# Releasing the first loads of w1 and of batch 1's q by k's features, casting the end of batch 0's v on two engines, and moving batch 7's q transposes, in an attention-and-mixer kernel on one core

## The chip, the core and the metric

The kernel runs on one core of a Trainium2 chip. The core has a matrix engine (TensorE, PE in the profile, with weight loads as PEld), three elementwise engines (VectorE, DVE; ScalarE, ACT; GpSimd, POOL) and an engine that only issues transfers and waits (SyncE, SP). Sixteen DMA engines move data for all of them. The metric is device time in microseconds (us), the median of several runs of the whole kernel.

## What is computed

The reference is a cosine-reweighted linear attention, whose output goes through a low-rank token mixer and a two-layer channel network. Eight batches, eight heads, 576 positions, head width 64, model width 512.

```
r      = relu(x);  phi(x) = [r * cos_w, r * sin_w]       # for q and k, cos_w/sin_w by position
kv     = sum over s of phi(k)[s, f] * v[s, d]            # per batch and head, 128 x 64
z      = sum over s of phi(k)[s, f]
x      = (phi(q) @ kv) / (phi(q) @ z + 1e-6)             # 576 x 512 per batch, heads side by side
u      = x + (x^T @ U @ V)^T                             # rank 32 over the positions
out    = u + relu(u @ w1) @ w2                           # w1 512 x 2048, w2 2048 x 512
```

Inputs and output are float32; the kernel multiplies in bfloat16.

## The kernel before, in words

**Tiles.** A batch's 576 positions are laid out nine to a pair of partitions, so that four chunks of 128 rows and one tail of 64 rows (chunk 4) come from two loads: the odd partitions' rows (`load_odd`, L80 in the profile) and the even partitions' rows with the tail (`load_even`, L74). q, k and v of a batch have one float32 staging tile each (`qst`, `kst`, `vst`), which the next batch's load overwrites. A `*_prep` turns a staged chunk into the two halves of its features (`scaled_relu`, L305 on ScalarE and L307 on VectorE).

**Order.** The order of the instructions on each engine is that of the program text; waits come from the data. Batch 0 is written out by hand. It runs q's features and their transposes on TensorE, k's features with the sums `z` (L1215), and then `first_chain` (L1269): casts of v to bfloat16, `kv` by pairs of heads (`kv0_mm`, L353, heads 0 to 3; `kv_unit`, L341, heads 4 to 7), the denominators (`den_mm`, L1223), the normalised x, the low-rank update and the transposed u. Multiplications with zeros fill TensorE's idle time at the start (`keep_warm`, L202). After that come numbered slots, each holding a unit of TensorE's work of the channel network; the attention work of the following batches is hung beside the slots (`beside`, `attention_plan`). `starts[b]` is the first slot of batch b.

**Loads around the change.** SyncE first issues batch 0's q, k and v, v in two halves of four heads. GpSimd issues the weights: w1 in four quarters of 512 columns (`w1_load`, L102; quarter n serves the hidden blocks 4n to 4n + 3), w2 likewise (`w2_load`, L108), each cast to bfloat16 on the way. A transfer is held back by a mark: a tiny copy that reads a tile, placed ahead of the transfer on the same engine, so that the engine waits until that tile is written.

- L1352, on GpSimd: reads q's tail features (`q_tl`); behind it w1's first quarter.
- L1354, on SyncE: a two-byte transfer that reads chunk 0 of k's cosine features; behind it batch 1's q.
- L1358, on GpSimd: reads the transposed tail of q; behind it w1's other quarters.
- L1361, on SyncE: reads `z_sb`; behind it batch 1's k and v.
- L1380, on GpSimd, slot 6: reads batch 1's transposed q; behind it w2.

After `first_chain` the channel network begins with six multiplications with w1's first quarter (`g1_open`, L727), then `g1_main` (L710). Between them batch 1's q is featured (`q_prep(1, ...)`) and transposed on TensorE (`qtr_unit`, L382).

**Later batches.** From batch 2 on q and u are transposed by the DMA engines, issued from SyncE: `qtr_dma` (L413 for the tail, L408 for two chunks at a time) and `utr_dma` (L535 for two quarters of u at a time, L541 for the tails). In `attention_plan(b)` F is the slot at which the features of batch b begin, G is `starts[b - 1]`, `at_q` gives the slots of the three transposes of q (tail, chunks 0 and 1, chunks 2 and 3), and `u_at + 2` and `u_at + 4` those of u. For batch 7, F is the first slot of batch 5's product with w2; batch 6's u is formed and its transposes are issued beside the same product. `uT_form` (L608) is VectorE's first use of a transposed u, `x_unit` (L439) TensorE's use of a transposed q.

Of the kernel before, what the change touches and what calls it, by code (L numbers as in the profile page):

```python
# [17 lines left out]
def kernel(  # L18
# [11 lines left out]
    nc = tc.nc  # L30

    B = 8
    H = 8
# [15 lines left out]
    def tail(b):  # L49
# [16 lines left out]
    qst, kst, vst = (  # L66
        pool.tile([P, H, 5, D], FP32, tag=n, bufs=1, name=n) for n in ("qst", "kst", "vst")
    )
# [43 lines left out]
    def cast(eng, o, i):  # L112
        if eng is nc.scalar:
            nc.scalar.activation(out=o, in_=i, func=AF.Copy, bias=0.0, scale=1.0)  # L114
        else:
            eng.tensor_copy(out=o, in_=i)  # L116


    V_, A_, G_ = nc.vector, nc.scalar, nc.gpsimd
# [15 lines left out]
    v0 = pool.tile([P, H, 5, D], BF16, tag="hid", bufs=1, name="v0")  # L135

    def load_uv():
# [16 lines left out]
        out=iota[:, 0:4], pattern=[[2, 4]], base=0, channel_multiplier=9,  # L154
        allow_small_or_imprecise_dtypes=True,
    )
    for lo in (0, TS):
        nc.gpsimd.iota(
            out=iota[lo : lo + TS, 4:5], pattern=[[1, 1]], base=8, channel_multiplier=18,
# [3 lines left out]
        out=iota[:, 5:6], pattern=[[1, 1]], base=8, channel_multiplier=9,  # L163
# [6 lines left out]
        out=par, in_=ident[:, 1:P:2], op=ALU.add, axis=mybir.AxisListType.X  # L170
# [14 lines left out]
    q_tl = const.tile([P, H, 2 * D], BF16)  # L185
# [943 lines left out]
    def attention_plan(b):  # L1129
        plan = []  # L1130
        odd = b % 2 == 1

        def put(at, f, *a):
            plan.append((at, lambda: f(b, *a)))

        ops = [(f, c, i) for f in (q_prep, k_prep) for c in QORD for i in range(2)]
        if b == 2:
            for n, (f, c, i) in enumerate(ops):
                if n < 8:
                    put((25, 26, 27, 28, 28, 29, 29, 30)[n], feature, f, c, i, A_)  # L1140
                elif n < 10:
                    put(24 + n, feature, f, c, i, V_)
                else:
                    put(
                        (34, 34, 35, 36, 37, 38, 39, 39, 40, 41)[n - 10], feature, f, c, i,
                        A_ if n in (14, 17) else V_,
                    )
            V0 = 33
            at_q, at_load = (32, 34, 36), (37, 42, 43)
            kv_at, x_at, a_at, u_at = 43, (44, 46, 48, 50, 52), 54, 55  # L1150
            a_bank = O1
        else:
            F, G = starts[b - 2] + (20 if odd and b < B - 1 else 16), starts[b - 1]
            late = b in (4, 6)
            both = (0, 1, 2, 8) if late else (0, 1, 2, 10, 11, 12) if b > 3 else (1, 2, 10, 11, 12)
            for s_ in range(G - F + 2 * late):
                for eng in (A_, V_)[: 1 + (s_ in both)]:
                    if ops:
                        put(F + s_, feature, *ops.pop(0), eng)
            V0 = starts[b - 2] + 9 if b > 3 else F + 1  # L1160
            at_q, at_load = (F + 7, F + 8, F + 8) if late else (F + 5, F + 7, F + 7), (F + 8, F + (16 if late else 14), V0 + (8 if late else 5))
            if b == 6:
                at_q, at_load = (F + 7, F + 12, F + 12), (F + 12, F + 16, V0 + 8)
            if b == 3:
                at_q = (F + 6, F + 7, F + 8)
                at_load = (F + 11, F + 14, F + 14)
            X0 = G - 2 if odd else G
            x_at = [
                X0 + i for i in ((2, 4, 6, 9, 11) if b == 3 else (2, 4, 6, 8, 10) if odd else (3, 5, 7, 9, 11))
            ]  # L1170
            kv_at = X0
            if late:
                kv_at, x_at = G + 3, [G + i for i in (5, 8, 13, 16, 18)]
            elif b - 1 in FULL:
                kv_at, x_at = G + 1, [G + i for i in ODDX]
            elif b - 1 in MIXED:
                kv_at, x_at = G + 1, [G + i for i in X5]
            a_at = x_at[4] + (3 if b in (4, 6) else 2)
            u_at = a_at + 1
            a_bank = T1 if b == 3 else OB  # L1180
        for n, c in enumerate(QORD):
            put(V0 + n, v_prep, 0, H, (c,), (G_,))
        for at_, (c0, c1) in zip(at_q, ((4, 5), (0, 2), (2, 4))):
            put(at_, qtr_dma, c0, c1)
        put(kv_at, kv_pair, *X1)
        for n, c in enumerate(ORD):
            put(x_at[n], x_unit, c, *((O1, X1)[n % 2] if b < 4 else X1))
        put(a_at, A_unit, *a_bank, A_)
        put(u_at, u_va, (0, *X1), (2, *O1) if b < 4 else (2, OA, OB))
        d0 = 2 if odd and b - 1 in FULL else 0  # L1190
        put(u_at, u_add, d0)
        put(u_at + 2, u_add, 2 - d0)
        put(u_at + 2, utr_dma, d0, d0 + 2)
        put(u_at + 4, utr_dma, 2 - d0, 4 - d0)
        if odd:
            late_t = 3 if b == 5 and b - 1 in FULL else 0 if b - 1 in FULL else 1 if b - 1 in MIXED else 0
            put(*((u_at + 1, u_tail, *T1) if b < 4 else (u_at + 3 + d0 + late_t, u_tail, *X1S)))
            put(u_at + 4 + d0 + late_t, utr_dma, 4, 5)
        if b < B - 1:
            for at_, t in zip(at_load, loads(b + 1)):  # L1200
                plan.append((at_, t))
        return plan
# [17 lines left out]
    def den_mm(b, d, cs):  # L1220
        for c in cs:
            for h in range(H):
                nc.tensor.matmul(  # L1223
                    out=d[:, c, h, :], lhsT=qT_of(b, c, h),
                    rhs=z_sb[:, h : h + 1].to_broadcast([P, 12]), start=True, stop=True,
                )
# [42 lines left out]
    def first_chain(b, xz, z, v_ps):  # L1269
        def fill(n):  # L1270
            for _ in range(n):
                nc.tensor.matmul(
                    out=xz[:, 1, P:512], lhsT=zero[:, 0:P], rhs=zero[:, 0:384],
                    start=True, stop=True,
                )

        d = xz[:, 1, 0:480].rearrange("p (c h n) -> p c h n", h=H, n=12)
        rec = pool.tile([P, 5, H], FP32, tag="rec5", bufs=1, name="rec5")
        cast(V_, v0[:, 0:2], vst[:, 0:2])
        cast(V_, z_sb, z[:, :, 0])  # L1280
        cast(V_, v0[:, 2:4], vst[:, 2:4])
        cast(V_, v0[:, 4:H], vst[:, 4:H])
        qtr_evac(b, 4, A_, t_q[4])
        kv_sb[b] = pool.tile([P, H, E], BF16, tag="kv", bufs=2, name="kv")
        acc = bank([P, 4, D], FP32, *G3, "kv_ps")
        kv0_mm(b, acc, (0, 1))
        den_mm(b, d, (0, 1, 2))
        kv0_mm(b, acc, (2, 3))
        cast(A_, V_bf, v_ps.rearrange("r (c p) -> r c p", c=4))
        cast(A_, kv_sb[b][:, 0:4, 0:D], acc)  # L1290
        den_mm(b, d, (3, 4))
        recip(rec, d[:, :, :, 0])
        x0 = [xh_mm(b, c, 0, *G3) for c in ORD[0:2]]
        kv_unit(b, 1, *T1, A_)
        x0 += [xh_mm(b, c, 0, *t) for c, t in zip(ORD[2:5], (G3, OA, OB))]
        xh_norm_act(b, ORD[4], 0, rec, x0[4])
        for n in range(4):
            xh_norm(b, ORD[n], 0, rec, x0[n])
        x1 = [xh_mm(b, c, 4, *t) for c, t in zip(ORD[0:4], (G3, G3, G3, T1))]
        for n in range(2):  # L1300
            xh_norm(b, ORD[n], 4, rec, x1[n])
        uT_alloc(b)
        a_ps = xz[:, 1, 0:P]
        a_mm(b, a_ps, (0, 1), range(5))
        cast(A_, A_of(b)[0:TS, :], a_ps[0:TS, :])
        for i, (tag, bufs) in enumerate((OA, OB, T1)):
            uT_ps[b, i] = bank([P, 4, P], FP32, tag, bufs, "uT_ps")
        for i in range(2):
            open_mm(b, i, uT_ps[b, i], range(4))
        x1.append(xh_mm(b, ORD[4], 4, *G3))  # L1310
        for n in range(2, 5):
            xh_norm(b, ORD[n], 4, rec, x1[n])
        for i in range(2):
            uTd_mm(b, i)
        for i in range(2):
            uTd_evac(b, i, A_)
        a2 = bank([P, P], FP32, *G3, "a_ps")
        a_mm(b, a2, (2, 3), range(5))
        cast(V_, A_of(b)[TS:P, :], a2[TS:P, :])
        open_mm(b, 2, uT_ps[b, 2], range(4))  # L1320
        u3 = ps.tile([P, 2, 512], FP32, tag="X", bufs=1, name="u3")
        uT_ps[b, 3] = u3[:, 0, :].rearrange("p (c t) -> p c t", c=4)
        open_mm(b, 3, uT_ps[b, 3], range(4))
# [25 lines left out]
        z_mm(0, c, z)  # L1349
    qtr_evac(0, 3, A_, t_q[3])  # L1350

    G_.tensor_copy(out=mark[0:1], in_=q_tl[0:1, 0, 0:1])  # L1352
    w1_load(0)
    nc.sync.dma_start(out=mark2, in_=k_p[0][0:1, 0, 0, 0:1])  # L1354
    load_odd(qst, q, 1)
    load_even(qst, q, 1)
    first_chain(0, xz, z, v_ps)
# [136 lines left out]
```

## Time and profile before

| what | us |
|---|---|
| three runs | 290.35, 290.05, 291.34 |
| median | 290.35 |
| profiled execution | 290.51 |
| its span in the profile | 288.7 |
| busy: TensorE, VectorE, ScalarE, GpSimd | 283.0, 218.9, 175.5, 70.9 |

The profile is of one execution; its span runs from the first to the last instruction that the profile counts, and the execution's own time is 1.8 us longer. Rows of a timeline give the start, the busy time, the engine (SPq is the transfer queue that SyncE feeds), the line, the operation, the tile written and the tile read, the shapes and how many instructions were merged; a bracket gives idle time of the engine before it and what ended it. Rows of a DMA queue give packets, megabytes and the packets' time as a share of sixteen engines over the window. The granted TensorE clock was 0.999 of full speed.

### The profile page before, as it was taken

The page shows a single profiled execution, that of the slowest core. Times are in us where ns is not written, and L with a number is a line of the kernel's source. Part 1 is how long each engine was busy: PE and PEld are TensorE (multiplying, and loading weights), DVE is VectorE, ACT ScalarE, POOL GpSimd, SP SyncE. Part 2 cuts the span into 40 slices and gives each one's busy share as a digit, 9 for nine tenths or more (in the row PEclk, how much of TensorE's full clock was granted, in tenths as well). Part 3 has the DMA queues.
Part 4 walks back from the last instruction along what each step waited for, and adds up shares of the span by engine and source line. Part 5 has one row for each costly group of instructions (what it writes and reads, how often), then busy time and mean ns, then how long its engine had stood idle before and what let it go on. Part 6 is the DMA issues. An engine that isn't in the chain of part 4 may idle for free.

```text
span 288.7 us, 7553 instructions
## 1 busy us (share of the span) xinstructions
PE 283.0 (98%) x3110; PEld 209.6 (73%) x3110; DVE 218.9 (76%) x446; ACT 175.5 (61%) x308; POOL 70.9 (25%) x111
## 2 busy tenths in 40 slices
PE   8999999999999999999999999999999999999995
PEld 6776455545887646886887667876888778899884
DVE  4979738887886677558895388958898689689864
ACT  2955661476687366986587488776795772177110
POOL 8340600040045304441006500351006000400140
PEclk9999999999999999999999999999999999999999
DMA  6999999999959898899829993599978200620023
GB/s 197 339 284 253 287 209 259 276 211 176 299 156 177 226 360 174 212 275 299 218 38 185 298 290 105 61 213 207 260 141 147 93 1 8 150 83 2 0 88 132
DMA packets 85447, 53.32 MB, mean 185 GB/s; under 512 B 53990, under 2 KB 83078, under 8 KB 85414
## 3 DMA queue, kind: packets, MB, share of 16 engines
q1 hardware_dynamic: 78998, 41.62, 60.0%
q0 software_dynamic: 6272, 11.17, 16.2%
q8 instruction: 24, 0.39, 0.6%
q10 hardware_dynamic: 144, 0.07, 0.1%
q14 instruction: 9, 0.07, 0.1%
HBM read 36.86 MB, written 9.44 MB: 160 GB/s over the span
## 4 chain that ended last, share of the span: by engine, by line
PE 92%; DMA 3%; DVE 2%; SPq 1%; issue 0%; DVEq 0%
PE w_ps L892 30%; PE g_ps L710 24%; PE al_ps L653 7%; PE be_ps L653 5%; PE gt_ps L741 5%; PE o_ps L781 5%; DMA vst<-in_v_dram 3%; PE x_ps L439 3%; PE kv_ps L364 3%; PE ot_ps L801 2%; PE ot_ps L994 2%; PE a_ps L465 1%; PE va_ps L495 1%; PE t_ps L382 1%; PE g_ps L727 0%; PE va_ps L518 0%
## 5 line engine op out<-in xcount | busy, mean ns | idle before, releaser
L710 PE MATMUL g_ps<-uT,w_bf 128*128 128x512 bf16 x314 | 77.0, 379 | 0.0
L717 ACT ACTIVATE hid<-g_ps 128x512 bf16<-128x512 f32 x80 | 47.4, 597 | 31.8 <-PE g_ps L710 26.6
L912 POOL TENSOR_TENSOR o_sb<-o_sb,u_bf 128x512 f32<-128x512 f32 x21 | 26.2, 1259 | 111.9 <-DVE o_sb L912 111.9
L710 PEld LDWEIGHTS <-w_bf 128*128 128x128 bf16 x314 | 29.1, 98 | 25.9
L892 PEld LDWEIGHTS <-hid 128*128 128x128 bf16 x448 | 43.1, 98 | 5.6 <-DVE hid L857 0.2
L678 DVE TENSOR_TENSOR hid<-pw,be_ps 128x512 bf16<-128x512 f32 x36 | 24.7, 686 | 17.0 <-PE be_ps L653 10.0
L892 PEld LDWEIGHTS <-S 128*128 128x128 bf16 x336 | 32.2, 98 | 4.5
L114 ACT ACTIVATE pw<-al_ps 128x512 f32<-128x512 f32 x36 | 21.3, 595 | 16.5 <-PE al_ps L653 8.9
L892 PE MATMUL w_ps<-T,hid 128*128 128x256 bf16 x224 | 27.9, 273 | 0.0
L892 PE MATMUL w_ps<-w_bf,hid 128*128 128x256 bf16 x224 | 27.6, 273 | 0.0
L892 PE MATMUL w_ps<-T,S 128*128 128x256 bf16 x224 | 27.1, 273 | 0.0
L114 ACT ACTIVATE o_sb<-w_ps 128x512 f32<-128x512 f32 x21 | 12.5, 597 | 20.5 <-PE w_ps L892 14.1
L912 DVE TENSOR_TENSOR o_sb<-o_sb,w_ps 128x512 f32<-128x512 f32 x21 | 14.3, 683 | 12.0 <-ACT o_sb L114 7.6
L506 DVE TENSOR_TENSOR u_bf<-x_bf,va_ps 128x1024 bf16<-128x1024 bf16 (+1 forms) x20 | 19.5, 998 | 3.4 <-PE va_ps L495 2.7
L653 PEld LDWEIGHTS <-sa 128*128 128x128 bf16 x192 | 17.7, 98 | 4.0 <-issue 0.2
L449 DVE TENSOR_TENSOR x_bf<-x_ps,rec 128x512 bf16<-128x512 f32 x28 | 19.3, 691 | 1.0
L305 ACT ACTIVATE k_p<-kst,sinw 128x512 bf16<-128x512 f32 x26 | 17.8, 713 | 0.1
L653 PEld LDWEIGHTS <-w_bf 128*128 128x128 bf16 x144 | 14.0, 98 | 3.5
L116 POOL CAST v_ext<-vst 128x512 bf16<-128x512 f32 x24 | 14.7, 652 | 7.1 <-issue 3.2
L741 PE MATMUL gt_ps<-uT_tl,w_bf 128*128 128x128 bf16 x256 | 16.4, 219 | 0.0
L781 PE MATMUL o_ps<-w_bf,hid 128*128 128x512 bf16 x64 | 15.6, 379 | 0.0
L741 PEld LDWEIGHTS <-w_bf 128*128 128x128 bf16 x256 | 15.0, 98 | 0.4
(191 smaller groups left out, 499.9 us busy)
## 6 DMA issues: line engine op xcount, KB each, us to landing
qst<-in_q_dram SPq DMA_DIRECT2D x14, 512.0 KB, 6.8
kst<-in_k_dram SPq DMA_DIRECT2D x14, 512.0 KB, 8.6
vst<-in_v_dram SPq DMA_DIRECT2D x12, 512.0 KB, 8.4
out_dram<-o_sb POOLq DMA_DIRECT2D x12, 512.0 KB, 5.4
w_bf<-in_moe_w_ch_dram POOLq DMA_DIRECT2D x8, 512.0 KB, 10.9
out_dram<-o_sb SPq DMA_DIRECT2D x4, 512.0 KB, 3.0
qst<-in_q_dram SPq DMA_DIRECT2D x2, 640.0 KB, 5.9
kst<-in_k_dram SPq DMA_DIRECT2D x2, 640.0 KB, 13.6
```

The source lines that it names most:

```text
L114: nc.scalar.activation(out=o, in_=i, func=AF.Copy, bias=0.0, scale=1.0)
L305: nc.scalar.activation(out=o, in_=i, func=AF.Relu, bias=0.0, scale=w)
L449: nc.vector.tensor_tensor(out=x_of(b, c, rows).rearrange("p (g i d) -> p g i d", g=2, d=D), in0=view[:, :, :, 0:D], in1=rec[rows].unsqueez ...
L506: nc.vector.tensor_tensor(out=u_bf[b][:, d0 : d0 + n], in0=x_bf[b].rearrange("p c (d n) -> p d c n", n=P)[:, d0 : d0 + n], in1=t.rearrange ...
L653: nc.tensor.matmul(out=res[:, k_, :], lhsT=lhs[:, d, k_, :], rhs=rhs[:, d, :], start=(opens and k_ == 0 and d == 0), stop=(k_ == 1 and d = ...
L678: V_.tensor_tensor(out=o, in0=x, in1=res, op=ALU.add)
L710: nc.tensor.matmul(out=g_ps.rearrange("p (c t) -> p c t", c=4), lhsT=w1_bf[:, d, j * P : j * P + P], rhs=uT[b][:, d, :, :], start=(d == 0) ...
L717: nc.scalar.activation(out=hid[b][:, j, :], in_=g_ps, func=AF.Relu, bias=0.0, scale=1.0)
L741: nc.tensor.matmul(out=g_ps[:, jj, :], lhsT=w1_bf[:, d, j * P : j * P + P], rhs=uT_tl[pr][:, d, :], start=(d == 0), stop=(d == 3),)
L781: nc.tensor.matmul(out=o, lhsT=hid[0][:, j, cc * P : cc * P + P], rhs=w2_bf[:, j, :], start=(j == 0), stop=(j == NJ - 1),)
L892: nc.tensor.matmul(out=res[:, g, :], lhsT=lhs[:, k_, g * P : g * P + P], rhs=rhs[:, k_, :], start=(opens and k_ == 0 and g == 0), stop=(k_ ...
L912: eng.tensor_tensor(out=o_, in0=x, in1=y, op=ALU.add)
```

## The change

Four edits:

1. In `first_chain`, VectorE casts heads 4 and 5 of batch 0's v; heads 6 and 7 are cast by ScalarE, after its copy of `kv` for heads 0 to 3 and ahead of its copy for heads 4 to 7.
2. The mark ahead of w1's first quarter reads chunk 0 of k's cosine features instead of q's tail features.
3. The mark ahead of batch 1's q reads chunk 1 of k's cosine features instead of chunk 0.
4. For batch 7 the transposes of q's four chunks are issued at slot F + 11 instead of F + 7; on SyncE they come behind the two transposes of batch 6's u instead of ahead of them. The transpose of q's tail stays at F + 5.

The numbers of instructions on TensorE, VectorE, GpSimd and SyncE stay; ScalarE has one more.

```diff
             at_q, at_load = (F + 7, F + 8, F + 8) if late else (F + 5, F + 7, F + 7), ...
+            if b == 7:
+                at_q = (F + 5, F + 11, F + 11)
             if b == 6:
...
     def first_chain(b, xz, z, v_ps):
...
         cast(V_, v0[:, 2:4], vst[:, 2:4])
-        cast(V_, v0[:, 4:H], vst[:, 4:H])
+        cast(V_, v0[:, 4:6], vst[:, 4:6])
         qtr_evac(b, 4, A_, t_q[4])
...
         cast(A_, kv_sb[b][:, 0:4, 0:D], acc)
+        cast(A_, v0[:, 6:H], vst[:, 6:H])
         den_mm(b, d, (3, 4))
...
-    G_.tensor_copy(out=mark[0:1], in_=q_tl[0:1, 0, 0:1])
+    G_.tensor_copy(out=mark[0:1], in_=k_p[0][0:1, 0, 0, 0:1])
     w1_load(0)
-    nc.sync.dma_start(out=mark2, in_=k_p[0][0:1, 0, 0, 0:1])
+    nc.sync.dma_start(out=mark2, in_=k_p[0][0:1, 1, 0, 0:1])
     load_odd(qst, q, 1)
     load_even(qst, q, 1)
     first_chain(0, xz, z, v_ps)
```

## The prediction

> **What bounds the kernel now.** I read the page first, then who waited on TensorE, the chain that ended last, and the first 40 us instruction by instruction, with the DMA queues in half-microsecond windows beside them.
>
> ```profile
> span 288.7 us, 7553 instructions
> PE 283.0 (98%) x3110; PEld 209.6 (73%) x3110; DVE 218.9 (76%) x446; ACT 175.5 (61%) x308; POOL 70.9 (25%) x111
> ```
>
> TensorE is busy 98% of the span. Its waits, in total, times and longest:
>
> ```profile
> PE w_ps L202 <- DVE zero L125: 1.2, 1, 1.2
> PE t_ps L394 <- ACT q_p L305: 0.4, 1, 0.4
> PE kv_ps L341 <- DVE v L116: 0.4, 1, 0.4
> ```
>
> All three lie before 17 us; the second half of v (heads 4 to 7) is the last. The chain names what stands behind it:
>
> ```profile
> 6.06 9.86 DMA vst<-in_v_dram
> ```
>
> So a microsecond won or lost in the first 24 us moves the end by as much, as long as no later transfer becomes late; after that TensorE's order is closed up, and an edit there can only cost.
>
> The timeline around the three head edits (start, busy, engine, line; a bracket is idle time before it):
>
> ```profile
> 10.40 0.81 POOL L102 DMA_DIRECT2D w_bf<-in_moe_w_ch_dram  x1
> 11.34 1.26 DVE L307 TENSOR_SCALAR k_p<-kst,cosw 128x512 bf16<-128x512 f32 x3
> 12.70 0.64 SPq L80 DMA_DIRECT2D qst<-in_q_dram  x1
> 13.74 1.00 ACT L114 ACTIVATE q_pT<-t_ps 128x1024 bf16<-128x1024 bf16 x1
> 15.63 0.39 ACT L114 ACTIVATE kv<-kv_ps 128x256 bf16<-128x256 f32 x1
> 15.81 2.80 POOL L102 DMA_DIRECT2D w_bf<-in_moe_w_ch_dram  x3 [0.29 <-issue]
> 16.01 0.83 DVE L116 CAST v<-vst 128x1280 bf16<-128x1280 f32 x1 [1.11 <-DMA vst<-in_v_dram]
> 16.75 0.19 DVE L429 TENSOR_SCALAR rec<-xz 128x40 f32<-128x40 f32 x1
> 16.89 0.29 PE L341 MATMUL kv_ps<-v,k_p 128*128 128x64 bf16 x4 [0.41 <-DVE v L116]
> 17.68 0.39 ACT L114 ACTIVATE kv<-kv_ps 128x256 bf16<-128x256 f32 x1 [1.66 <-PE kv_ps L341]
> 21.70 1.47 PE L727 MATMUL g_ps<-uT,w_bf 128*128 128x512 bf16 x6
> 22.33 0.71 ACT L305 ACTIVATE q_tl<-qst,sinw 128x512 bf16<-128x512 f32 x1
> 23.87 0.61 PE L382 MATMUL t_ps<-ident,q_tl 128*128 128x128 bf16 x8
> ```
>
> To be seen: the cast of v ends at 16.84 and TensorE starts heads 4 to 7 at 16.89; at 21.70 the first multiplication with w1 needs w1's first quarter; at 23.87 TensorE transposes batch 1's q, made from the load of 12.70.
>
> The DMA queues (packets, MB, share of 16 engines) in the windows 13 to 13.5, 14 to 14.5, 15 to 15.5, 16.5 to 17, 19 to 19.5 and 23 to 23.5 us, a fence each, then three issues with the time to their landing. q1 is SyncE's queue, q0 GpSimd's, q8 fetches instructions.
>
> ```profile
> q1 hardware_dynamic: 137, 0.17, 99.4%
> q8 instruction: 1, 0.02, 14.2%
> q0 software_dynamic: 6, 0.01, 7.2%
> ```
>
> ```profile
> q0 software_dynamic: 94, 0.10, 115.2%
> ```
>
> ```profile
> q1 hardware_dynamic: 7, 0.01, 5.9%
> ```
>
> ```profile
> q1 hardware_dynamic: 177, 0.18, 101.8%
> ```
>
> ```profile
> q8 instruction: 1, 0.02, 14.1%
> ```
>
> ```profile
> q0 software_dynamic: 60, 0.06, 72.0%
> q1 hardware_dynamic: 60, 0.06, 44.2%
> ```
>
> ```profile
> w_bf<-in_moe_w_ch_dram POOLq DMA_DIRECT2D x1, 512.0 KB, 8.3
> vst<-in_v_dram SPq DMA_DIRECT2D x1, 320.0 KB, 9.9
> qst<-in_q_dram SPq DMA_DIRECT2D x1, 512.0 KB, 7.2
> ```
>
> w1's first quarter, issued at 10.40, moves its first packets just before 13.5, 3.0 us later, as v runs out. From 14 it has the engines (0.10 MB in half a microsecond) until batch 1's q has them (0.18 MB at 16.5 to 17). So today the two take turns. v's last packets drip on until 15.5, seven in that half microsecond: the fetch of 13 to 13.5 held one engine for 14.2% of 16 x 0.5 = 1.1 us. They land at 6.06 + 9.9 = 16.0, half a microsecond after the last packet.
>
> **The change part by part.**
>
> *The two casts.* VectorE's 0.83 us for four heads becomes half of it, and ScalarE takes heads 6 and 7 right after its copy of 15.63, from 16.02. The trace has no ScalarE cast of 128x640 from SBUF: 128x512 took 0.71 (row of 22.33), 128x1024 took 1.00 (row of 13.74). I take 0.80, near the first: done at 16.82. Heads 4 and 5 fill TensorE's hole before that. Four heads take 17.68 - 16.89 = 0.79, two about 0.45; so heads 6 and 7 end at 16.87 + 0.45 = 17.3 in place of 17.65, 0.3 us earlier (0.1 to 0.45 by the two ends). VectorE reaches `rec` 0.4 us earlier. Behind the new wait of ScalarE stands only its next copy, which needs the same heads. The chain to 21.70 follows both engines without a gap that it could hide in: **-0.3**, w1 wanted at 21.4.
>
> *w1's first quarter.* Its mark now reads k's first cosine features, done at about 11.8 (three in 1.26 from 11.34), in place of q's last. POOL issues it at about 12.0, 1.6 us later, and by the 3.0 us above its packets come at 15.0. v then shares with nobody; but the engine that fetched instructions still has v's packets to do, and ScalarE isn't free before 16.02 anyway. An earlier v gains nothing beyond the 0.3: only the half on VectorE could start sooner. Behind the waiting mark stand, on GpSimd, only w1's later quarters, whose own release comes at 15.81.
>
> [...]
>
> *Batch 1's q.* Its gate waits for k's second cosine features, 0.4 us later: issue at 13.1. Behind the gate stand on SyncE only q's two loads and the gate of k. No packet of an unhindered load shows its lead there; the first load of the run (issued at 0.73) showed packets from 2.2 on, so 1.5 us:
>
> ```profile
> q1 hardware_dynamic: 19, 0.02, 77.0%
> ```
>
> (window 2 to 2.5). q's packets come at about 14.6. **Between v's end near 14.0 and 14.6 the engines have little to do, and then q and w1 want them together.** Together they are 1.18 MB at 0.18 per half microsecond, 3.3 us, and 0.52 MB at 0.10, 2.6 us: 5.9 us from 14.6, so 20.5. In the window 19 to 19.5 the next fetch takes an engine for another 1.1 us; today both loads are nearly through by then (18.7 and 19.9 for the rows above), afterwards they are not. 20.5 + 1.1 + 0.5 to land is 22.1. TensorE wants w1 at 21.4: it waits 0.7. Against 21.70 that is **+0.4**; without the fetch's 1.1 it would be -0.3, with q and w1 worse shared up to +2 (below). I take +0.4. q at 22.1 still meets ScalarE's 22.33.
>
> *Batch 7's transposes.* SyncE issues them behind batch 6's of u:
>
> ```profile
> 210.92 4.38 SPq L408 DMA_TRANSPOSE q_pT<-q_p  x2
> 213.23 2.41 DVE L506 TENSOR_TENSOR u_bf<-x_bf,va_ps 128x1024 bf16<-128x1024 bf16 x3
> 215.41 3.61 SPq L535 DMA_TRANSPOSE uT<-u_bf  x2
> 220.95 0.42 DVE L608 TENSOR_TENSOR tb<-uT 128x512 bf16<-128x512 bf16 x1
> 235.16 0.42 PE L439 MATMUL x_ps<-kv,q_pT 128*128 128x65 bf16 x8
> q_pT<-q_p SPq DMA_TRANSPOSE x12, 5.5
> ```
>
> u's first transpose can go when the first add is done, near 214.5 in place of 215.41. Its first user, VectorE at 220.95, has no bracket: it doesn't wait today, so nothing is gained. q's two end their issue near 215.7 + 1.8 + 4.4 = 222; with 5.5 to land, 227.5, and the second half is read at 235.16. **0**, with 7 us of cover; SyncE has nothing else queued until batch 7's u. If it did go wrong, TensorE would wait in batch 7's x.
>
> *The sum:* -0.3 at the casts, +0.7 of waiting for w1, 0 in batch 7: +0.4 on the profiled execution's 290.51 (288.7 and 1.8 around it), 290.9. The median of the three runs, 290.35, lies 0.16 lower: **290.75**.
>
> **The rivals.**
>
> *q starves (slower).* GpSimd's queue goes on after the first quarter: its next quarters are issued from 15.81, so at 18.8 to 19 the second stands behind the first without a break. The window 23 to 23.5 shows how two full queues divide: 60 packets each, 0.06 MB. If q shares so from 15.0 on, its remaining 1.0 MB take 7.1 to 8.3 us (0.07 to 0.06 MB each half), to 22.1 or 23.3; with 0.5 to land and 1.1 for a fetch, 23.7 to 24.9. ScalarE's features (0.71) then release TensorE at 24.5 to 25.7 instead of 23.87: +0.6 to +1.8, about +1.2, **291.55**. It decides once q lands later than about 23.1. The shared window speaks for it; against it, that q gets there first and has half a microsecond alone. [...]
>
> *The head's gain survives.* If both loads are there by 21.4 (no engine held up, w1 served first), TensorE opens 0.3 early. But it meets w2's first quarter:
>
> ```profile
> 30.60 2.97 POOL L108 DMA_DIRECT2D w_bf<-in_moe_w_ch_dram  x4 [0.28 <-issue]
> w_bf<-in_moe_w_ch_dram POOLq DMA_DIRECT2D x1, 512.0 KB, 8.2
> 38.86 1.03 PE L781 MATMUL o_ps<-w_bf,hid 128*128 128x512 bf16 x4
> ```
>
> It lands at 38.8 and is read at 38.86. The DMA engines are full until then, so an earlier issue lands hardly earlier: half of the gain goes. -0.15: **290.2**.
>
> *The change does not do what it says:* v lands no earlier, since the fetch and not w1 makes it late. Then the casts still run as above and the sum is the same; it needs no number of its own.
>
> **How the numbers follow.** The forecast, an end moved by 0 to +0.8, has 0.45; the starved q 0.30; the surviving gain 0.20; 0.05 is for a stall that I don't see. Measuring tells about 0.5%, 1.45 us, from no change: 288.9 to 291.8. Nothing here gains 1.45 us: faster 0.03. The starved q passes 291.8 in about half of its cases, and with the rest that makes slower 0.20; same 0.77. The range runs from the surviving gain with a little more (290.0) to the upper end of the starved q (292.2).
>
> **What would show it.** Right: VectorE's cast of two heads, ScalarE's of two done at 16.8, the kv copy at 17.4; w1 and q moving together from 15 on; w1's first multiplication near 22.0 with a wait on w1's DMA; no change of gaps from 200 us on. The starved q: the transposes of batch 1's q at 24.5 or later, behind features that wait for the load. The surviving gain: 21.4 at w1 and a wait at 38.8. Wrong altogether: v lands before 14.5 and TensorE has heads 6 and 7 before 16.5, or TensorE waits in batches 6 or 7.

## The result and the profile after

The changed kernel takes 291.48 us (median of 15 runs, 290.98 to 292.08); the kernel before, run beside it, 290.80 (15 runs, 290.05 to 291.81). The ratio is 1.003, with an interval of 1.0018 to 1.0042: about 0.9 us slower (the medians alone are 0.68 apart). The profiled execution took 291.50 us against 290.51, so the two traces show the whole of it. The forecast was 290.75 and a stall of TensorE at w1. The size was too small, and the stall is somewhere else; that 291.48 still lies inside the range that was given, 290.0 to 292.2, is luck.

The page of the changed kernel, its waits of TensorE, and its chain of work that ended last:

```profile
span 289.7 us, 7554 instructions
PE 283.5 (98%) x3110; PEld 209.6 (72%) x3110; DVE 218.4 (75%) x446; ACT 176.2 (61%) x309; POOL 71.5 (25%) x111
```

```profile
PE t_ps L382 <- ACT q_tl L305: 1.2, 1, 1.2
PE t_ps L394 <- ACT q_p L305: 0.2, 1, 0.2
```

```profile
13.77 10.11 DMA qst<-in_q_dram
```

The wait for v's second half (0.4 us before) is gone, a wait of 1.2 us at the transposes of batch 1's q is new, and the chain, which went through v's load, now goes through the second of q's two loads: issued at 13.77, landed at 23.88. No wait for w1 is listed.

The same rows of the timeline as those shown of before:

```profile
12.13 0.81 POOL L102 DMA_DIRECT2D w_bf<-in_moe_w_ch_dram  x1
13.04 0.64 SPq L80 DMA_DIRECT2D qst<-in_q_dram  x1
...
15.67 0.49 DVE L116 CAST v<-vst 128x640 bf16<-128x640 f32 x1 [0.62 <-DMA vst<-in_v_dram]
...
16.08 0.73 ACT L114 ACTIVATE v<-vst 128x640 bf16<-128x640 f32 x1
...
16.48 0.28 PE L341 MATMUL kv_ps<-v,k_p 128*128 128x64 bf16 x4
...
17.34 0.39 ACT L114 ACTIVATE kv<-kv_ps 128x256 bf16<-128x256 f32 x1 [0.54 <-PE kv_ps L341]
...
21.25 1.47 PE L727 MATMUL g_ps<-uT,w_bf 128*128 128x512 bf16 x6
...
23.96 0.72 ACT L305 ACTIVATE q_tl<-qst,sinw 128x512 bf16<-128x512 f32 x1 [1.98 <-DMA qst<-in_q_dram]
...
24.74 0.62 PE L382 MATMUL t_ps<-ident,q_tl 128*128 128x128 bf16 x8 [1.15 <-ACT q_tl L305]
```

Read down TensorE's rows against those of before: 16.48 against 16.89 (0.41 earlier), 21.25 against 21.70 (0.45 earlier), 24.74 against 23.87 (0.87 later). Between these two executions everything up to w1's first use is a gain (e8 below tells how little of it can be put down to the change); between w1 and the transposes of q it turns into a loss of 1.3 us, and the row of 23.96 says why: ScalarE stood idle for 1.98 us until q had landed. ScalarE's cast of two heads took 0.73 us (forecast 0.80).

The DMA queues of the changed kernel at 14 to 14.5, 16.5 to 17, 18 to 18.5 and 22 to 22.5 us, a fence each (packets, MB, share of 16 engines):

```profile
q0 software_dynamic: 10, 0.01, 57.3%
q1 hardware_dynamic: 1, 0.00, 1.9%
```

```profile
q0 software_dynamic: 98, 0.10, 121.9%
q1 hardware_dynamic: 1, 0.00, 0.7%
```

```profile
q1 hardware_dynamic: 177, 0.18, 102.9%
q0 software_dynamic: 7, 0.00, 5.7%
```

```profile
q1 hardware_dynamic: 60, 0.06, 44.7%
q0 software_dynamic: 58, 0.06, 69.6%
```

Four phases: hardly a packet (11 in half a microsecond); w1's first quarter alone; q alone; q's last pieces and w1's second quarter half and half. So w1 and q, which the forecast had share from 15 on, take turns, and w1 has the first.

How much the engines lost is seen in the totals of a longer window, 13 to 15 us of before and of the changed kernel, then 12 to 39 us of both:

```profile
DMA packets 453, 0.50 MB, mean 252 GB/s; under 512 B 17, under 2 KB 452, under 8 KB 452
```

```profile
DMA packets 226, 0.27 MB, mean 135 GB/s; under 512 B 16, under 2 KB 225, under 8 KB 225
```

```profile
DMA packets 6885, 7.30 MB, mean 270 GB/s; under 512 B 261, under 2 KB 6881, under 8 KB 6881
```

```profile
DMA packets 6576, 7.00 MB, mean 259 GB/s; under 512 B 246, under 2 KB 6572, under 8 KB 6572
```

The later releases leave the engines half empty for 2 us (0.27 MB in place of 0.50, at a busy share of 0.69 in place of 1.19), and by 39 us they are 0.30 MB behind; at the 0.27 MB per microsecond of before that is an estimated 1.1 us. The load that TensorE needs next in that stretch is w2's first quarter, and TensorE takes it up as soon as it is there (issue with the time to landing; TensorE's first product with it):

```profile
31.48 2.98 POOL L108 DMA_DIRECT2D w_bf<-in_moe_w_ch_dram  x4 [0.28 <-issue]
```

```profile
w_bf<-in_moe_w_ch_dram POOLq DMA_DIRECT2D x1, 512.0 KB, 8.3
```

```profile
39.85 1.02 PE L781 MATMUL o_ps<-w_bf,hid 128*128 128x512 bf16 x4
```

31.48 + 8.3 = 39.8, and 39.85 is 0.99 later than the 38.86 of before. In this trace w2 was also issued 0.88 later than before (30.60), since its mark reads q's transposes, so the trace alone doesn't tell the late issue from the backlog of the engines; e11 does. From there on nothing changes any more. Batch 7's part, SyncE and TensorE from 215 to 229 us, then TensorE's row of before:

```profile
215.45 2.76 SPq L535 DMA_TRANSPOSE uT<-u_bf  x2
218.32 5.67 SPq L408 DMA_TRANSPOSE q_pT<-q_p  x2
...
228.85 0.42 PE L439 MATMUL x_ps<-kv,q_tlT 128*128 128x65 bf16 x8
```

```profile
227.87 0.42 PE L439 MATMUL x_ps<-kv,q_tlT 128*128 128x65 bf16 x8
```

u's transposes now go ahead of q's, and are issued some 0.9 us sooner relative to TensorE; TensorE's first x of batch 7 stands at 228.85 against 227.87 in before, again 0.98 later. The end is 1.0 later. The fourth edit has moved nothing that TensorE sees.

### The profile page after: what moved, and what is told of

The parts are those of the page before. It is cut to its first block, busy times and chain, and to the rows that moved or that the text cites. A ratio compares the mean times of both kernels' runs of the same rounds, so it can differ in the third digit from the quotient of the medians.

```text
span 289.7 us, 7554 instructions
## 1 busy us (share of the span) xinstructions
PE 283.5 (98%) x3110; PEld 209.6 (72%) x3110; DVE 218.4 (75%) x446; ACT 176.2 (61%) x309; POOL 71.5 (25%) x111
## 3 DMA queue, kind: packets, MB, share of 16 engines
HBM read 36.86 MB, written 9.44 MB: 160 GB/s over the span
## 4 chain that ended last, share of the span: by engine, by line
PE 90%; DMA 6%; ACT 1%; DVE 1%; issue 0%; ACTq 0%; DVEq 0%
PE w_ps L892 30%; PE g_ps L710 23%; PE al_ps L653 7%; PE be_ps L653 5%; PE gt_ps L741 5%; PE o_ps L781 5%; DMA qst<-in_q_dram 3%; PE x_ps L439 3%; DMA kst<-in_k_dram 3%; PE kv_ps L364 3%; PE ot_ps L801 2%; PE ot_ps L994 2%; PE va_ps L495 1%; PE a_ps L465 1%; PE t_ps L382 1%; ACT k_p L305 1%
## 5 line engine op out<-in xcount | busy, mean ns | idle before, releaser
L114 ACT ACTIVATE pw<-al_ps 128x512 f32<-128x512 f32 x36 | 21.3, 595 | 16.5 <-PE al_ps L653 8.9
L114 ACT ACTIVATE o_sb<-w_ps 128x512 f32<-128x512 f32 x21 | 12.5, 597 | 20.5 <-PE w_ps L892 14.0
L506 DVE TENSOR_TENSOR u_bf<-x_bf,va_ps 128x1024 bf16<-128x1024 bf16 (+1 forms) x20 | 19.5, 999 | 3.4 <-PE va_ps L495 2.6
L116 POOL CAST v_ext<-vst 128x512 bf16<-128x512 f32 x24 | 16.3, 718 | 7.3 <-DMA vst<-in_v_dram 4.0
```

The lines of the kernel that those rows point to most:

```text
L506: nc.vector.tensor_tensor(out=u_bf[b][:, d0 : d0 + n], in0=x_bf[b].rearrange("p c (d n) -> p d c n", n=P)[:, d0 : d0 + n], in1=t.rearrange ...
```

## The experiments

Three theories of why q is late. **A**: the queues take turns; whichever of w1's first quarter and q reaches idle engines first runs through, so q's landing follows w1's release. **B**: q is late by its own gate, 0.35 us later. **C**: q is late because it shares with w1's second quarter. A fourth came up with the first four runs. **D**: what TensorE can win before 38.9 us is cut off at w2's first quarter.

| label | kernel | median us | before us | ratio and interval |
|---|---|---|---|---|
| e1_w1_early | w1's release as before | 290.72 | 290.45 | 1.0001 [0.9978, 1.0025] |
| e2_q_early | q's release as before | 291.78 | 290.45 | 1.0025 [1.0003, 1.0047] |
| e3_releases_only | only the two releases | 291.48 | 290.45 | 1.0032 [1.0013, 1.0052] |
| e4_casts_and_b7 | only casts and batch 7 | 290.36 | 290.45 | 0.9984 [0.9966, 1.0001] |
| e5_w2_early | e4 and w2 sooner | 290.64 | 290.32 | 1.0015 [0.9987, 1.0043] |
| e6_w1_later | w1 still later | 294.52 | 290.32 | 1.0157 [1.0135, 1.0179] |
| e7_q_first | q ahead of w1 | 290.87 | 290.32 | 1.0017 [1.0007, 1.0027] |
| e8_b7_only | only batch 7's move | 290.95 | 290.32 | 1.0022 [1.0005, 1.0038] |
| e9_w1_rest_later | w1's second quarter later | 296.20 | 290.38 | 1.0206 [1.0183, 1.0229] |
| e10_casts_only | only the casts | 290.35 | 290.38 | 1.0009 [0.9988, 1.0031] |
| e11_no_b7 | without batch 7's move | 291.34 | 290.38 | 1.0037 [1.0024, 1.0049] |
| e12_casts_w2 | casts and w2 sooner | 290.84 | 290.38 | 1.0009 [0.9991, 1.0027] |

"Before" is the kernel before, run beside each; the ratio has its 95% interval. The diffs are against the changed kernel, unless said otherwise.

### e1_w1_early: w1's release undone

```diff
-    G_.tensor_copy(out=mark[0:1], in_=k_p[0][0:1, 0, 0, 0:1])
+    G_.tensor_copy(out=mark[0:1], in_=q_tl[0:1, 0, 0:1])
     w1_load(0)
```

> The changed kernel with one edit undone: w1's first quarter is again released by q's tail features, some 1.7 us earlier. Theory A (turns: of w1's quarter and batch 1's q, the one that reaches the idle DMA engines first runs through, the other follows it, so q's landing follows w1's release): w1 takes its turn from 13.4 as before, q from 15.9, q's last landing is near 22.2 in place of 23.9, the 1.2 us wait of batch 1's transposes is gone, and the head's 0.4 us stays: ratio to the kernel before 0.9985 to 0.9995. Theory B (q is late because its own gate is 0.35 us later): q lands little earlier than in the changed kernel, 23.5, wait 0.8 us, ratio 1.002. Theory C (q is late because it shares with w1's second quarter at the end): that quarter still comes at 19 to 20, so the last landing stays above 23 and the ratio at 1.002 to 1.003.

w1 is issued at 10.70 and q at 13.75, 0.7 later than in the changed kernel, as its head ran late. The wait at q's transposes is gone all the same:

```profile
23.92 0.61 PE L382 MATMUL t_ps<-ident,q_tl 128*128 128x128 bf16 x8
```

w1's queue went first (184 packets to 16 of SyncE's from 14 to 15), then SyncE's (292 to 50 from 16 to 17). q was issued later and landed sooner: B falls, and C as it stands, for w1's second quarter has the release of the changed kernel. The loss of time is gone too (1.0001); its TensorE reads w2 at 39.15, just when that lands (30.65 + 8.5). A stands.

### e2_q_early: q's release undone

```diff
     w1_load(0)
-    nc.sync.dma_start(out=mark2, in_=k_p[0][0:1, 1, 0, 0:1])
+    nc.sync.dma_start(out=mark2, in_=k_p[0][0:1, 0, 0, 0:1])
```

> The changed kernel with batch 1's q released again by the first chunk of k's features (0.35 us earlier), w1's first quarter late as in the change. Theory A: w1 still reaches the engines first (its packets began at 14.2, q's could not before 14.2 to 14.6), so q still goes second: last landing 23.5 to 23.9, ratio 1.002 to 1.003. If q should get there first, A says that q lands near 20 and w1's quarter near 21, ratio 0.999. Theory B: the wait goes down by 0.35 us or more, ratio 1.001 or less. Theory C: no difference to the change, 1.003.

With q's old gate the kernel is as slow as the changed one (1.0025): B falls again. In its profile w1 was issued at 13.13, q at 13.64; the windows show 98 packets of w1's queue to none of q's at 16.5 to 17, and 179 of q's to three at 18.5 to 19, the same turns. That execution took 293.36, 1.6 over its median, so its places are not used further.

### e3_releases_only: no casts, no batch 7

```diff
-        cast(V_, v0[:, 4:6], vst[:, 4:6])
+        cast(V_, v0[:, 4:H], vst[:, 4:H])
...
-        cast(A_, v0[:, 6:H], vst[:, 6:H])
...
-            if b == 7:
-                at_q = (F + 5, F + 11, F + 11)
```

> Only the two later releases (w1's first quarter and batch 1's q by k's features), with the single cast of v on VectorE and batch 7 as before. Theory A: v lands at 15.6 in place of 16.0, the cast of 0.83 us starts there, TensorE has heads 4 to 7 some 0.3 us earlier, and all of that is lost in the wait for q at 23.9: ratio 1.003, as in the whole change. The rival that the extra work on ScalarE costs something further on: ratio 1.000 to 1.001, since the casts are as before.

1.0032: the two releases carry the whole loss. TensorE waits 0.83 us at q's transposes and 0.18 for w2.

### e4_casts_and_b7: the releases undone

```diff
-    G_.tensor_copy(out=mark[0:1], in_=k_p[0][0:1, 0, 0, 0:1])
+    G_.tensor_copy(out=mark[0:1], in_=q_tl[0:1, 0, 0:1])
...
-    nc.sync.dma_start(out=mark2, in_=k_p[0][0:1, 1, 0, 0:1])
+    nc.sync.dma_start(out=mark2, in_=k_p[0][0:1, 0, 0, 0:1])
```

> Only the two casts and the order of batch 7's transposes; both releases as before. The casts are worth 0.3 us at w1's first multiplication (21.4 in place of 21.7). Theory A: q lands at 22.2 as before, its features start 0.1 to 0.2 us later than the engines are free, and 0.2 to 0.3 us remain: ratio 0.999. Rival (the forecast's cap: w2's first quarter lands at 38.8, when TensorE wants it): the gain is gone by 39 us, ratio 1.000, with a wait of TensorE at the first product with w2.

290.36 against 290.45 (0.9984, an interval that just holds 1). TensorE opens w1 at 21.24, 0.46 sooner than before, and arrives at w2 with that lead, where it ends:

```profile
38.89 1.02 PE L781 MATMUL o_ps<-w_bf,hid 128*128 128x512 bf16 x4 [0.33 <-DMA w_bf<-in_moe_w_ch_dram]
```

38.89 against 38.86: from here on this execution stands where that of before stood. This is what theory D says. Without the bracket one wouldn't see that the execution of before, too, is at that limit: its w2 landed at 38.8. But e10, with the same casts and releases, has no such wait, and a gain of 0.45 us would be a ratio of 0.9985: the 0.9984 can't tell a gain that was lost from one that was kept.

### e5_w2_early: e4, and w2 released two steps sooner

The diff is against e4.

```diff
-        G_.tensor_copy(out=mark[0:1], in_=q_pT[1][0:1, 3, 0, 0:1])
+        G_.tensor_copy(out=mark[0:1], in_=q_pT[1][0:1, 1, 0, 0:1])
...
-    at(6, w2_all)
+    at(4, w2_all)
```

> The two casts and batch 7's transposes as in the change, the two releases as before, and w2's quarters released two steps sooner, by batch 1's q of chunk 1 in place of chunk 3. Theory D (the casts' gain of 0.45 us reaches 38.9 and is lost there because w2's first quarter lands at 38.8): w2's first quarter lands 1 to 2 us sooner, TensorE does not wait at o_ps, the 0.45 us stay to the end; ratio to the kernel before 0.9985 or a little below (0.9975 to 0.9990), about 290.0. Rival (the DMA engines are full until 39, so an earlier release lands no earlier, or it makes batch 1's or 2's loads late): TensorE waits at o_ps as before, or at the next kv for v, and the ratio is 1.000 to 1.003.

Inconclusive. 1.0015 speaks against a gain, but its one profile fell on an execution (293.83) in which TensorE waited 1.9 us for batch 0's first q and then ran at a lower clock (0.74 from 10 to 12 us and 0.50 from 12 to 14; last section), so that it came to w2 only at 40.90 and found it landed. e12 is the same test again.

### e6_w1_later: w1 released by k's last features

```diff
-    G_.tensor_copy(out=mark[0:1], in_=k_p[0][0:1, 0, 0, 0:1])
+    G_.tensor_copy(out=mark[0:1], in_=k_p[0][0:1, 3, 0, 0:1])
     w1_load(0)
```

> All of the change, but w1's first quarter is released by k's last chunk of cosine features, so that it is issued about 1.7 us later than in the changed kernel (near 13.9) and q near 13.0 as there. Theory A (whichever load reaches the idle engines first runs through, the other follows): q's packets start near 14.7, q lands by 18 to 20, w1's first quarter follows and lands at 20.5 to 22.5; the wait at batch 1's transposes of q (0.87 us in the changed kernel) is gone, and TensorE waits 0 to 1 us at w1's first use instead; w2 then hides up to half a microsecond; ratio 1.000 to 1.002. Theory B (q is late because of its own gate): q lands as in the changed kernel, 22.5 to 23.9, and the time is 1.003. Theory C (q shares with w1's quarters packet by packet): both land after 20.5 and the transposes of q wait again by 0.3 us or more, 1.002 to 1.004.

The order turned round, as A says: q (issued at 13.70, w1 at 14.77) had the engines first (189 packets of its queue to none of w1's at 17 to 17.5, w1's first 15 at 18.5 to 19), landed before ScalarE asked for it at 22.49, and TensorE waited for w1 instead:

```profile
22.49 0.71 ACT L305 ACTIVATE q_tl<-qst,sinw 128x512 bf16<-128x512 f32 x1
...
23.79 1.77 PE L727 MATMUL g_ps<-uT,w_bf 128*128 128x512 bf16 x6 [1.86 <-DMA w_bf<-in_moe_w_ch_dram]
```

But 1.86 us of waiting cost 4.2 us in all by the medians (1.0157), which no theory had. The windows of 24 to 28 us say where the rest went; the column after the five engines is the granted clock of TensorE:

```profile
22.00:24.00 2.00, 0.21 (x1) 0.11 (x2) 2.00 (x5) 1.20 (x2) 0.00 (x0) 1.00 1.17 249
24.00:26.00 2.00, 2.00 (x8) 0.84 (x7) 0.64 (x2) 0.00 (x0) 0.00 (x0) 0.70 1.17 255
26.00:28.00 2.00, 2.00 (x12) 1.24 (x11) 0.00 (x0) 1.19 (x2) 0.00 (x0) 0.50 1.15 262
```

By these windows, and 0.94 from 28 to 30, TensorE lost 0.30, 0.50 and 0.06 of its clock for 2 us each, 1.7 us in all, which is an estimated 3.4 us at the 0.50 of 26 to 28; its products of 512 columns started 0.43 us apart (four from 25.36 to 27.07) in place of 0.22 (four from 28.96 to 29.82). The wait was paid nearly twice.

### e7_q_first: q released by batch 0's last q

```diff
     w1_load(0)
-    nc.sync.dma_start(out=mark2, in_=k_p[0][0:1, 1, 0, 0:1])
+    nc.sync.dma_start(out=mark2, in_=q_tl[0:1, 0, 0:1])
```

> All of the change, but q is released by batch 0's own last features of q, so that it is issued near 11 to 12, straight behind v; w1's first quarter at 12.1 as in the changed kernel. Theory A: q stands in the queue before v is through and has the engines first or w1 has them for one turn; either way q is through by 20 to 21.5 and the transposes of q do not wait; w1's first quarter lands by 18 to 21.3; what is left is the casts' gain, cut off at w2's first quarter near 38.9: ratio 0.9985 to 1.000. Theory B: the same. Theory C: q shares with w1 and lands at 22 to 24 as in the changed kernel, ratio 1.002 to 1.004. Another risk: q in the queue beside v makes v's second half late, then kv of batch 0 waits and the head loses 0.3 us or more.

q was issued at 10.83, w1 at 12.00. Two windows, 15 to 15.5 and 18 to 18.5:

```profile
q1 hardware_dynamic: 150, 0.18, 108.4%
```

```profile
q0 software_dynamic: 99, 0.10, 121.2%
q1 hardware_dynamic: 3, 0.00, 2.5%
```

At 15, three microseconds after its issue, w1 has not one packet: q goes first, and right behind v, so that the engines are never empty (0.71 MB between 13 and 15). C, as a sharing of the whole load, falls here too. The wait is at w1 now: 507 of some 512 packets of its first quarter came between 16 and 19.5, and the last of it landed at 22.1 (10.1 us after its issue). An instruction fetch near 19.5 took one engine for 0.9 us (11.8% of sixteen over half a microsecond) and may have held it back; the trace doesn't name the engine.

```profile
22.13 1.47 PE L727 MATMUL g_ps<-uT,w_bf 128*128 128x512 bf16 x6 [0.95 <-DMA w_bf<-in_moe_w_ch_dram]
```

1.0017, between before and the changed kernel, and not the gain that A let hope for.

### e8_b7_only: the fourth edit alone

The diff is against the kernel before.

```diff
+            if b == 7:
+                at_q = (F + 5, F + 11, F + 11)
```

> Batch 7's transposes of q alone are moved behind batch 6's of u. The forecast's step and every theory: nothing, ratio 1.000 within 0.002; TensorE's instructions from 200 us on stand where they stood. If the move is worth something that the other edits hide, the ratio leaves 0.998 to 1.002 and TensorE's position shifts between 215 and 240 us.

The ratio, 1.0022 [1.0005, 1.0038], leaves the range that was expected, though its trace shows nothing: the profiled execution took 290.14, shorter than that of before, TensorE is never idle from 200 us on, and its runs scatter from 290.14 to 292.35. e10 and e11 tell whether the move costs anything.

The trace shows something else. Up to 200 us this is the kernel before, with its single cast of four heads and its early releases, and yet:

```profile
21.29 1.47 PE L727 MATMUL g_ps<-uT,w_bf 128*128 128x512 bf16 x6
```

v's second half landed near 15.5 here in place of 15.9, and VectorE's cast began at 15.58 in place of 16.01; TensorE started heads 4 to 7 at 16.50, without a wait, in place of 16.89. So TensorE opens w1 0.41 sooner than in the trace of before without any change in the head, and the 21.25 of the changed kernel and the 21.24 of e4 are only 0.04 and 0.05 sooner than that. What the casts are worth can't be read from two traces.

### e9_w1_rest_later: w1's second quarter kept away from q

```diff
-    G_.tensor_copy(out=mark[0:1], in_=q_tlT[0:1, 0, 0:1])
+    G_.tensor_copy(out=mark[0:1], in_=x_bf[0][0:1, ORD[1], 4 * D : 4 * D + 1])
     for n in range(1, 4):
         w1_load(n)
```

> The changed kernel, but w1's second to fourth quarter are released by the second chunk's x of heads 4 to 7 (done near 19) in place of batch 0's last q, so that the second quarter is issued at 19.5 instead of 15.8 and has no packet beside q's. What makes q's last three pieces land 1 to 2 us behind the other thirteen in the changed kernel? If the second quarter beside them (theory C in its small form): all of q lands by 22.3, the wait at its transposes falls from 0.87 to under 0.3 us. If the turn behind w1's first quarter and the instruction fetch near 19.5 alone (theory A): the pieces still land at 23 or later and the wait stays at 0.6 us or more. The total can lose elsewhere: the second quarter then lands near 25.5 to 26.5, where TensorE first reads it at about 26, so a wait for w1 of 0 to 1 us may come in; ratio 1.001 to 1.005.

With no packet of w1 beside its last pieces q lands at 22.6 and TensorE doesn't wait for it (its transposes at 23.71 have no bracket). That looks like C's small form, by which part of q's lateness in the changed kernel is the sharing of its last pieces. But e11 below leaves the sharing as it is in the changed kernel, and q lands at 22.5 there: one trace of each doesn't tell the sharing from scatter, and the cause of q's late last pieces stays open. The price of the edit is elsewhere: the second quarter, issued at 19.95, now stood behind batch 1's k and v and landed 10.5 us later.

```profile
30.50 1.54 PE L710 MATMUL g_ps<-uT,w_bf 128*128 128x512 bf16 x4 [3.99 <-DMA w_bf<-in_moe_w_ch_dram]
```

Four microseconds of waiting, a granted clock of 0.50 from 32 to 34 behind it, and 5.8 us lost (1.0206; 1.005 at most was expected). The turn that was to be spared was lost to two other loads.

### e10_casts_only and e11_no_b7: is it the fourth edit?

e10 against the kernel before, then e11 against the changed kernel:

```diff
-        cast(V_, v0[:, 4:H], vst[:, 4:H])
+        cast(V_, v0[:, 4:6], vst[:, 4:6])
...
+        cast(A_, v0[:, 6:H], vst[:, 6:H])
```

```diff
-            if b == 7:
-                at_q = (F + 5, F + 11, F + 11)
```

> The two casts alone. The casts' 0.45 us are won at 16.9 and reach 38.9, where w2's first quarter takes them back: ratio 0.9985 to 1.0005, and the same as with batch 7's move beside it. If batch 7's move costs something by itself (its single run gave 1.0022), this kernel is faster than the one that has both: ratio 0.996 to 0.998.

> The change without batch 7's move. Theory A: q is late as in the changed kernel, ratio 1.002 to 1.004. If batch 7's move costs 0.2 %: 1.000 to 1.001.

The casts alone give 290.35 against 290.38, the casts with the move (e4) 290.36 against 290.45; the change without the move has 1.0037, with it 1.003. The move costs nothing that these runs can tell, and e8's 0.2% is scatter, or at least no cause for it was found.

e10's trace goes against theory D. Its w2 was issued at 30.02 and landed at 38.1, and TensorE met it without a wait, 0.58 sooner than in before:

```profile
38.28 1.03 PE L781 MATMUL o_ps<-w_bf,hid 128*128 128x512 bf16 x4
```

The lead lasted to the end (289.95 against 290.51). e8, without the casts, did nearly as well: 38.45, and 290.14. So the cut at w2 that e4 shows isn't there in every execution, and by the medians (0.9984 in e4, 1.0009 here, each with an interval of about 0.002 to either side) the casts are worth something between nothing and their 0.45 us.

e11's trace holds more. q landed at 22.5 there, and TensorE did **not** wait at its transposes, so by A and C the loss should be gone. It isn't:

```profile
23.63 0.61 PE L382 MATMUL t_ps<-ident,q_tl 128*128 128x128 bf16 x8
```

```profile
39.61 1.02 PE L781 MATMUL o_ps<-w_bf,hid 128*128 128x512 bf16 x4 [0.82 <-DMA w_bf<-in_moe_w_ch_dram]
```

TensorE comes to the transposes 0.24 sooner than before, and then waits for w2 until 39.61, 0.75 later than before. w2 was issued at 30.36, also sooner than before (30.60), but took 9.2 us instead of 8.2. The engines had moved 7.01 MB from 12 to 39, as in the changed kernel (7.00). So w2 was late here with an early issue, which leaves the backlog as what made it late. q's wait is only the first place where the delay of the transfers can show; w2 is the second, and either gives the same end.

### e12_casts_w2: the casts, and w2 sooner, once more

The diff is against e10.

```diff
-        G_.tensor_copy(out=mark[0:1], in_=q_pT[1][0:1, 3, 0, 0:1])
+        G_.tensor_copy(out=mark[0:1], in_=q_pT[1][0:1, 1, 0, 0:1])
...
-    at(6, w2_all)
+    at(4, w2_all)
```

> The two casts, w2 released two steps sooner, nothing else. The profile is what is wanted, in an execution with an undisturbed head. Theory D: w2's first quarter lands before 38, TensorE does not wait at o_ps, its instructions stand 0.4 us earlier than before from 17 us to the end, ratio 0.9975 to 0.9990. Rival: the DMA engines are full until 39 and w2 lands when it did, or batch 1's v lands later and kv waits: TensorE's lead is gone by 42 us, ratio 0.999 to 1.002.

w2 is issued at 28.49, 2.1 sooner than before, and lands at 28.49 + 9.6 = 38.1, 0.7 sooner. TensorE meets it with its lead whole, as e10 did without the earlier release (38.30 against 38.28), and loses it 3 us on:

```profile
38.30 1.03 PE L781 MATMUL o_ps<-w_bf,hid 128*128 128x512 bf16 x4
...
40.23 0.70 DVE L116 CAST v_ext<-vst 128x1024 bf16<-128x1024 f32 x1 [3.60 <-DMA vst<-in_v_dram]
...
41.52 0.28 PE L341 MATMUL kv_ps<-v_ext,k_p 128*128 128x65 bf16 x4 [0.73 <-DVE kv L116]
```

It looks as if the bytes that w2 was given first were missing at batch 1's v, on which VectorE stood idle for 3.60 us (0.66 in e10, but 2.15 in e4, so part of it may be scatter); its cast and its copy of `kv` (at 41.05) then hold TensorE until 41.52, 0.33 later than in before. 1.0009 lies in the range of D's rival and above D's own. In e4 the lead ended at w2, in e12 at v, in e10 nowhere: the loads up to some 40 us can take back what is won in the head, and don't in every execution. No version among the twelve is faster than the kernel before by more than can be told; e4 is the nearest, at 0.9984.

## Why the prediction was right or wrong, point by point

**What bounds the kernel** was half right. TensorE's chain bounds the first 24 us, but the forecast read the DMA engines only for the loads that TensorE asks for next. They are full from 12 to 39 us (a busy share of 1.17 over it, 1.12 or more in each four microseconds), and w2's first quarter, the load that is needed next in that stretch, landed at 38.8 and was used at 38.86: in the profiled execution of before, the transfers and TensorE arrive together (in e8's, with the same loads, TensorE took w2 up at 38.45 without a wait). The rows of 8.2 and 38.86 stood in the prediction, and it used them only to cap a gain.

**The casts, -0.3**: right in kind, but not shown as a size. Between the two traces it is -0.41 at `kv` and -0.45 at w1's first use; against e8's trace, where v's second half landed 0.4 sooner and was cast as before, only -0.04. ScalarE's cast took 0.73 in place of 0.80.

**w1's first quarter**: this is the step that failed. "By the 3.0 us above its packets come at 15.0": its first came just before 14, under 2 us after its issue at 12.13, and it had the engines to itself until 17 and landed at 18.6. The 3.0 us of before weren't a lead; they were the lead and the wait for v's turn to end at 13.5 (868 packets of SyncE's queue from 10.4 to 13, none of w1's). e7 shows the same from the other side, 4 us from issue to first packets, behind q. "Then q and w1 want them together", from 14.6 on: they may both want them, but here they didn't share. w1 went through first and nearly alone (98 packets to one at 16.5 to 17), and q followed (177 to seven at 18 to 18.5). So the 0.7 us of waiting for w1 that make the forecast's sum weren't there (21.25, no bracket).

**q, landing at 22.1 without cost**: wrong, and this is the loss in the changed kernel's own trace. It began after 17 and landed at 23.88; its transposes came 0.87 late. The forecast had this place and nearly this time, 24.5 or later, in its rival "q starves", but by another mechanism (an even sharing from 15 on). e1, e6 and e7 show turns; what keeps q's last pieces back isn't shown (e9 against e11). And the margin was smaller than the forecast thought. The 19.9 that it took for q today is the landing of the first of q's two loads; the last piece of the second landed at 22.2 in before, 0.2 ahead of ScalarE's 22.33. The starved q's 291.55 is near the measured 291.48, which is luck as well.

**Batch 7, 0**: right; 0.98 before and behind it.

**The sum, +0.4**: measured about +0.9 by the ratio, and +0.99 in the profiled executions. Its largest term, +0.7 at w1, wasn't there, and the loss came from a term that it put at nothing, so that the sign is right by luck. "The engines have little to do" from 14.0 to 14.6 was written down and not charged. That gap, grown to 0.23 MB less between 13 and 15 us, is the loss: the queue of transfers is full from there to 39 (a busy share of 1.09 or more in each two microseconds from 16 on), so what isn't moved then comes late at a load that is needed, q or w2 (e11).

**"The head's gain survives", -0.15**: it needed the releases undone. For the casts alone e4's trace bears it out (-0.46 at 21.24, +0.03 at 38.89) and e10's doesn't (-0.58 at 38.28, kept to the end); the medians can't decide.

The rival "q starves" took the even division of the window 23 to 23.5 from the first packet on. Here w1's quarter, 512 KB in packets of about 1 KB (98 made 0.10 MB), so some 512 of them, had moved 438 before q's first 76 in 17 to 17.5; at 22 to 22.5 the same two queues are even, 60 to 58. So the trace shows one long turn at the start and an even division later; no run here tells what makes the difference.

## What to carry to other kernels

Where the DMA engines are full for a long stretch, ask of a release not only who needs the load but whether the engines stay fed: a transfer released 1.7 us later for a good reason left them half empty for 2 us (0.27 MB in place of 0.50), and the next load that was needed, up to 25 us on, came 1 us late. Don't take an interval from issue to first packet for a lead without looking for who held the engines: w1's was 3.0 us behind v in the kernel before, 4 behind q in e7 and under 2 in the changed kernel. And a gain ahead of such a stretch can be taken back by a load at its far end (e4), if not in every execution (e10): check where the next needed load lands against where it is used, even if no wait is shown there.

## What the runs showed of the hardware that was not expected

The longest waits of TensorE had a second price. 1.15 us (the changed kernel) and 0.95 (e7) left the granted clock at 1.00; 1.86 (e6), 1.94 (e5's profiled execution) and 3.99 (e9) were followed by two windows of 2 us at 0.70 to 0.74 and 0.50, and e6 and e9 lost 4.2 and 5.8 us by the medians. What a wait between 1.15 and 1.86 us does, and by what the clock is lowered, no run here shows.

GpSimd's casting load moved 0.10 MB in half a microsecond when alone, SyncE's plain load 0.18. But the profile counts the casting load as bfloat16: a quarter of w1 is 512 x 512 numbers, and it says 512 KB. They are read as float32: of the 36.86 MB that the page says were read from HBM, q, k and v make 28.31, U and V 0.15 and w1 and w2, at four bytes a number, 8.39; at two bytes the sum would be 32.65. Counted so the two rates are 0.20 and 0.18, and a quarter of w1 holds the engines an estimated 2.6 us (0.52 MB at the 0.10 that the profile counts), nearly as long as 1 MB of q (2.8 us at 0.18) and twice as long as its 512 KB suggest.

The fetches of instructions are single packets of 16 KB (24 of them 0.39 MB on the page) that took an engine for 0.9 us (11.8% of sixteen engines in half a microsecond, e7) to 1.1 us (14.2%, the kernel before). In the traces of before and of the changed kernel the last of the sixteen pieces of the second load of batch 1's q land some two microseconds behind most others: fifteen by 20.0 and the last at 22.2 in before, between 20.5 and 23.88 in the changed kernel, thirteen of them before 21.7. A fetch that holds one engine fits that, but the traces don't name the engines, and no run here shows it.
